# First eight units: v and q scaled three units ahead, one load queue, scores from scaled q with a mask

## The chip, the cores and the metric

One NeuronCore of a Trainium2 chip runs the whole program. The metric is the device time of one execution in microseconds, the median of the runs. The engines are TensorE (PE, with its weight loads as PEld), VectorE (DVE), ScalarE (ACT), GpSimd (POOL), and SP, which here only issues DMAs; each has its own queue of instructions and they meet through semaphores.

## The reference

Three parts, one after the other. A linear attention with decay on q, k, v of 4 batches, 8 heads, 768 positions, 64 dimensions:

```python
state = gamma * state + k[t] (outer) v[t]      # gamma = 1 - 2**(-5 - head)
y[t]  = q[t] @ state / sqrt(64)
```

Its output, 3072 tokens of 512, goes through `h = x @ w_in; g = h - tanh(h); y = g @ w_out` with 2048 inner columns, and that through a second such block with 1024 inner columns: `h = x @ w_in2`, softmax of h times h, a layer norm with the gain g_ln, and `@ w_out2`. All weights and the output are float32 on the outside; the weights of the first and second block come as float64 words, which the kernel turns into float32.

## The kernel before, in words

The attention is worked in chunks of 128 positions. Chunk c and batch b are one unit, k = 4c + b, so there are 24 units in six chunks, and a unit holds all 8 heads. Inside a unit the chunk is split in two halves of 64 positions. For each unit two tiles `z` of 512 KB come from memory: one with q and k, dimensions on the partitions, one with k and v, positions on the partitions. Decay is taken out of the recurrence by scaling: v is multiplied by gamma to the power of minus its position (`vs`, constants in `con`), q by gamma to the power of its position over 8 (`qs`, constants in a table `tab` of 256 KB per chunk). `prepare` makes both. `unit(ko, ks)` does the outputs of unit ko (`out`: scaled q against the states, L240 to L244, and the kept scores against v, L245 to L251) and the scores and state products of unit ks (`sc`: k against q, and k against v, L278 to L286). Scores go through VectorE into `pr`, where they are multiplied by a second table, which holds the decay and the causal mask at once (L290). States are `sa` and `sb`. The outputs are summed into `xf` (ScalarE copies L262 to L266, VectorE adds L268) and split into a high part rounded to the matmul format (`xh`, L306) and the low rest (`xl`, L307), in the tile `xt` of the chunk.

A matmul of float32 shows in the trace as two instructions; a score or output product is 64 x 64 by 64 columns, a product of the dense blocks 128 x 128 by 512 columns.

The first dense block works on one chunk of four units (512 tokens) at a time. `step_h(n, b)` takes column block n of 16 for chunk b: twelve matmuls `ph` (L319), tanh on ScalarE (L325), the difference on VectorE (L326). The weights of each block n are decoded from their words in four stages by the class Decoder: load (`raw`, SP's queue), absolute value on ScalarE (L121), four VectorE operations (L128 to L135), and the split into high and low (L144, L145). `dec1.to(stage, upto)` runs one stage up to a number of blocks.

The program for the first two chunks is at L382 to L412: units 0 to 7, with the scores two units ahead of the outputs, `prepare` two ahead, and one `step_h` at k = 4. Then the loop from L414 runs the h steps of chunks 0 and 1 with units 8 to 11 among them, then the y products (`py`, L343) of both chunks, then from L489 chunks 2 to 5, with the units 12 to 23 as visits between the steps (L494 to L500), and at last the second dense block.

Program order sets priorities; a list scheduler with its own model of times then orders each engine's queue, and moves loads forward where a buffer is free. Tiles come from two pools of equal buffers: `t4` (44 of 4 KB a partition: z, raw, w, xt, g) and `t2` (17 of 2 KB: vs, qs, tab, pr, xf, wf and others). `products` keeps the order of the small matmuls among themselves. In the kernel before, z, w_in and con are issued from SP's queue and the tables from ScalarE's.

Of the kernel before, what the change touches and what calls it, by code (L numbers as in the profile page):

```python
# [57 lines left out]

C_VS = 0
C_HALF = C_VS + NC * H  # L60
C_IDENT = C_HALF + 1
C_END = C_IDENT + P


# [5 lines left out]
def constants():  # L70
    gamma = 1.0 - 2.0 ** (-5.0 - np.arange(H, dtype=np.float64))
    i = np.arange(P, dtype=np.float64)
    out = np.zeros((P, C_END), np.float64)
    out[:, C_IDENT : C_IDENT + P] = np.eye(P)
    for c in range(NC):
        out[:, C_VS + c * H : C_VS + (c + 1) * H] = gamma[None, :] ** -(c * P + i[:, None] + 1)
    out[:, C_HALF] = -0.5

    tab = np.zeros((NC, 2, P, 4 * P), np.float64)
    of_score = tab[:, 0].reshape(NC, 2, D, 2, NP, D)  # L80
    of_q = tab[:, 1].reshape(NC, 2, D, NP, P)
    for p in range(NP):
        for h in range(2):
            for c in range(NC):
                t = gamma[2 * p + h] ** (c * P + i + 1) / np.sqrt(D)
                of_q[c, h, :, p, :] = t
                of_score[c, :, :, h, p, :] = t.reshape(2, 1, D) * (i[:D, None] <= i[None, :D])
    return out.astype(np.float32), tab.astype(np.float32)


# [1 line left out]
def body(ctx: ExitStack, tc, z, w_in, w_out, w_in2, w_out2, g_ln, cst, tab, out):  # L92
# [8 lines left out]
    def t4(shape, dtype, name):  # L101
        return big.tile(shape, dtype, tag="t4", name=name)

    def t2(shape, dtype, name):
        return mid.tile(shape, dtype, tag="t2", name=name)

    con = cpool.tile([P, C_IDENT], F32, name="con")
    gl = cpool.tile([P, NF2], F32, name="gl")
    mhalf = con[:, C_HALF : C_HALF + 1]
    y1d = [yd.tile([P, B, NK, P], F32, name=f"y1d{s}") for s in range(NSB)]  # L110


# [67 lines left out]
    xc = {}  # L180
    loaded = [0]

    def load_units(upto):
        while loaded[0] < min(upto, NU):
            k = loaded[0]
            if k % B == 0:
                tb[k // B] = [t2([P, NP * P], F32, "tab") for _ in range(2)]
                for n, t in enumerate(tb[k // B]):
                    nc.scalar.dma_start(out=t, in_=tab[k // B, n])
            for half, to in ((0, zq), (1, zv)):  # L190
                t = t4([P, 2, NP, P], F32, "z")
                nc.sync.dma_start(out=t.rearrange("p a b c -> p (a b c)"), in_=z[2 * k + half])
                to[k] = t
            loaded[0] += 1

    def rows(h):
        return slice(h * D, (h + 1) * D)
# [4 lines left out]
                nc.tensor.matmul(o, a, b, start=True, stop=True, skip_group_check=True)  # L202
            )

    def prepare(k, own):

        c = k // B
        v = t2([P, H, D], F32, "vs")
        src = zv[k][:, 1, :, :].rearrange("q p (h d) -> q (p h) d", h=2)
        c0 = C_VS + c * H  # L210
        for h in range(own):
            nc.scalar.activation(
                v[:, h, :], src[:, h, :], AF.Copy, scale=con[:, c0 + h : c0 + h + 1]
            )
        if own < H:
            nc.gpsimd.tensor_tensor(  # L216
                v[:, own:, :], src[:, own:, :],
                con[:, c0 + own : c0 + H].unsqueeze(2).to_broadcast([P, H - own, D]), ALU.mult,
            )
        vs[k] = v  # L220
        qs[k] = t2([P, NP, P], F32, "qs")
        nc.gpsimd.tensor_tensor(
            qs[k].rearrange("q p t -> q (p t)"),
            zq[k][:, 0, :, :].rearrange("q p t -> q (p t)"), tb[c][1], ALU.mult,
        )

    def unit(ko, ks, hold=False, pool=ps_r, tag="r", engs=None):


        if ko is not None:  # L230
            c, b = divmod(ko, B)
            q, v, po, st = qs.pop(ko), vs.pop(ko), pt.pop(ko), (sa.pop(ko, None), sb.pop(ko))
            w = [ps_r.tile([P, 2, 4 * D], F32, tag="r", name="out") for _ in range(2)]
            fr = [t[:, 0, :].rearrange("q (i t) -> q i t", i=2) for t in w]
            y = [t[:, 1, :].rearrange("q (h i t) -> q h i t", h=2, i=2) for t in w]

            steps = range(2) if c else (1,)
            products([
                (
                    fr[h][rows(col(2 * i + odd, h)), i, rows(ab)],  # L240
                    st[ab][rows(h), 2 * i + odd, :], q[rows(h), 2 * i + odd, rows(ab)],
                )
                for i in range(2) for ab in steps for odd in range(2) for h in range(2)
            ])  # L244
            products([  # L245
                (
                    y[ab][rows(col(p, h)), h, p // 2, :], v[rows(ab), 2 * p + h, :],
                    po[rows(ab), h, p, :],
                )
                for p in range(NP) for ab in range(2) for h in range(2)  # L250
            ])  # L251
            if hold:
                if b % 2 == 0:
                    xc[b // 2] = t4([P, 2, 2, 2, P], F32, "xc")
                xf = xc[b // 2][:, b % 2, :, :, :]
            else:
                xf = t2([P, 2, 2, P], F32, "xf")
            xa = xf.rearrange("q h i t -> q (h i) t")
            ya = [t.rearrange("q h i t -> q (h i) t") for t in y]
            if c:  # L260
                for h in range(2):
                    nc.scalar.copy(xf[:, h, :, :], fr[h])  # L262
            else:
                for h in range(2):
                    nc.scalar.copy(xf[:, h, :, rows(1)], fr[h][:, :, rows(1)])
                nc.scalar.copy(xa[:, :, rows(0)], ya[0])  # L266
            for ab in steps:
                nc.vector.tensor_tensor(  # L268
                    xa[:, :, rows(ab)], xa[:, :, rows(ab)], ya[ab], ALU.add
                )  # L270
            if not hold:
                split_x(c, b, xf, engs or (nc.gpsimd, nc.gpsimd))
        if ks is not None:
            c = ks // B
            kq, kv, v = zq[ks], zv.pop(ks), vs[ks]
            w = [pool.tile([P, 2, 4 * D], F32, tag=tag, name="sc") for _ in range(2)]
            sc, gn = ([t[:, n, :].rearrange("q (p t) -> q p t", p=NP) for t in w] for n in range(2))
            products([  # L278
                (sc[h][rows(ab), p, :], kq[rows(h), 1, p, rows(ab)], kq[rows(h), 0, p, rows(ab)])
                for p in range(NP) for h in range(2) for ab in range(2)  # L280
            ])
            zq.pop(ks)
            products([
                (gn[ab][rows(h), p, :], kv[rows(ab), 0, p, rows(h)], v[rows(ab), 2 * p + h, :])
                for p in range(NP) for ab in range(2) for h in range(2)
            ])  # L286
            pr = t2([P, 2, NP, D], F32, "pr")
            for h in range(2):
                f = tb[c][0].rearrange("q (h p t) -> q h p t", h=2, p=NP)[:, h, :, :]
                nc.vector.tensor_tensor(pr[:, h, :, :], sc[h], f, ALU.mult)  # L290
            pt[ks] = pr
            sb[ks] = stp.tile([P, NP, D], F32, tag="sb", name="sb", bufs=3)
            if c == 0:
                nc.scalar.copy(sb[ks], gn[0])
            else:
                nc.vector.tensor_tensor(sb[ks], sa[ks], gn[0], ALU.add)
            if c < NC - 1:
                sa[ks + B] = stp.tile([P, NP, D], F32, tag="sa", name="sa")
                nc.vector.tensor_tensor(sa[ks + B], sb[ks], gn[1], ALU.add)
# [80 lines left out]


    spare = dict(pool=ps_y, tag="y")  # L382
    both = dict(engs=(nc.vector, nc.gpsimd))
    dec1.n = NF1
    load_units(1)
    nc.sync.dma_start(out=con, in_=cst[:, :C_IDENT])
    load_units(2)
    dec1.to(0, 1)
    load_units(5)
    prepare(0, H // 2)  # L390
    unit(None, 0, **spare)
    prepare(1, H // 2)
    for st in range(1, 4):
        dec1.to(st, 1)
    unit(None, 1, **spare)
    g2 = {}

    def step_h(n, b):
        if b == 0:
            g2[n] = t4([P, 2, SB], F32, "g")  # L400
        less_tanh(products_h(b, n, ps_y, "y"), g2[n][:, b, :])

    for k in range(2 * B):
        load_units(min(k + 6, 2 * B))
        if k + 2 < 2 * B:
            prepare(k + 2, H // 2)
        if k == B:
            step_h(0, 0)
        unit(k, k + 2 if k + 2 < 2 * B else None, **both, **(spare if k < B else {}))
        if k >= B:  # L410
            dec1.to(0, k - B + 2)
    dec1.step()  # L412
    nc.sync.dma_start(out=gl, in_=g_ln)
    for n in range(NF1):  # L414
        while dec1.at[3] < n + 1:
            dec1.step()
        for b in range(2):
            if n or b:
                step_h(n, b)

        if LATER <= n <= LATER + B:
# [234 lines left out]
```

## Time and profile before

| | us |
|---|---|
| median of 3 runs | 909.95 (909.57 to 910.24) |
| the profiled execution's own time | 910.57 |
| its span (first to last instruction) | 908.8 |
| TensorE busy | 876.0 |

The span is 1.8 us less than the profiled execution's time; that execution was 0.62 us above the median. The rows further down are from this one execution; their times count from the start of the span. "Idle before, with a releaser" names what ended the wait of an engine; "issue" stands for time in which the engine waited for nothing that the profile shows.

### The profile page before, as it was taken

The page shows a single profiled execution, that of the slowest core. Times are in us where ns is not written, and L with a number is a line of the kernel's source. Part 1 is how long each engine was busy: PE and PEld are TensorE (multiplying, and loading weights), DVE is VectorE, ACT ScalarE, POOL GpSimd, SP SyncE. Part 2 cuts the span into 40 slices and gives each one's busy share as a digit, 9 for nine tenths or more (in the row PEclk, how much of TensorE's full clock was granted, in tenths as well). Part 3 has the DMA queues.
Part 4 walks back from the last instruction along what each step waited for, and adds up shares of the span by engine and source line. Part 5 has one row for each costly group of instructions (what it writes and reads, how often), then busy time and mean ns, then how long its engine had stood idle before and what let it go on. Part 6 is the DMA issues. An engine that isn't in the chain of part 4 may idle for free.

```text
span 908.8 us, 15882 instructions
## 1 busy us (share of the span) xinstructions
PE 876.0 (96%) x6656; PEld 724.9 (80%) x6656; DVE 429.9 (47%) x872; ACT 300.7 (33%) x605; POOL 195.9 (22%) x200
## 2 busy tenths in 40 slices
PE   5669999999999999999999999999999999999998
PEld 4558887888888888888888888888888888888886
DVE  3466876994223233222322259964544444444442
ACT  4435544652111112111211134522433333333332
POOL 3422000000044333333333310010322112222210
PEclk9779999999999999999999999999999999999999
DMA  9913203422411313110311046114111111000000
GB/s 357 408 77 116 72 25 118 138 72 90 116 47 57 107 48 94 48 60 11 100 41 47 25 128 196 48 38 136 31 40 46 47 47 46 24 24 24 24 25 35
DMA packets 35640, 73.47 MB, mean 81 GB/s; under 512 B 3184, under 2 KB 15600, under 8 KB 35568
## 3 DMA queue, kind: packets, MB, share of 16 engines
q1 hardware_dynamic: 17712, 56.73, 18.5%
q10 hardware_dynamic: 17856, 15.73, 5.5%
q8 instruction: 52, 0.85, 0.4%
q14 instruction: 20, 0.16, 0.1%
HBM read 59.86 MB, written 12.58 MB: 80 GB/s over the span
## 4 chain that ended last, share of the span: by engine, by line
PE 90%; issue 3%; DVE 2%; POOL 2%; ACT 2%; DMA 1%; POOLq 0%; DVEq 0%; ACTq 0%
PE ph L319 29%; PE py L343 26%; PE po L580 14%; PE ph L532 14%; PE ptr L567 2%; PE sc L202 2%; PE out L202 2%; POOL vs L216 1%; DVE g L326 1%; ACT th L325 1%; DMA z<-z 1%; POOL xl L307 1%; DMA tab<-tab 1%; DVE gh L333 0%; DVE xf L268 0%
## 5 line engine op out<-in xcount | busy, mean ns | idle before, releaser
L319 PE MATMUL ph<-xh,w 128*128 128x512 f32 x768 | 248.1, 392 | 5.3 <-ACT xh L306 4.9
L343 PE MATMUL py<-gh,w 128*128 128x512 f32 x768 | 248.2, 391 | 1.2 <-ACT gh L331 1.2
L319 PEld LDWEIGHTS ph<-xh,w 128*128 128x128 f32 x768 | 144.7, 188 | 36.5 <-ACT xh L306 5.3
L343 PEld LDWEIGHTS py<-gh,w 128*128 128x128 f32 x768 | 144.1, 188 | 32.1 <-ACT gh L331 1.6
L326 DVE TENSOR_TENSOR g<-ph,th 128x512 f32<-128x512 f32 x96 | 66.2, 690 | 196.4 <-ACT th L325 196.4
L319 PE MATMUL ph<-xl,w 128*128 128x512 f32 x384 | 150.3, 391 | 0.1
L343 PE MATMUL py<-gl,w 128*128 128x512 f32 x384 | 149.8, 390 | 0.0
L325 ACT ACTIVATE th<-ph 128x512 f32<-128x512 f32 x96 | 57.3, 599 | 257.4 <-PE ph L319 244.5
L532 PE MATMUL ph<-w,y 128*128 128x512 f32 x576 | 134.8, 389 | 0.0
L334 POOL TENSOR_TENSOR gl<-g,gh 128x512 fp32r<-128x512 f32 x48 | 61.8, 1287 | 329.3 <-DVE gh L333 305.3
L532 PEld LDWEIGHTS ph<-w,y 128*128 128x128 f32 x576 | 108.0, 188 | 22.4
L580 PE MATMUL po<-w,uh 128*128 128x512 f32 x384 | 120.4, 395 | 0.0
L378 POOL TENSOR_TENSOR y<-yl,y 128x512 fp32r<-128x512 f32 x24 | 42.2, 1759 | 260.9 <-ACT y L377 260.9
L538 DVE TENSOR_REDUCE nmx<-ph 128x1 f32<-128x1024 f32 x24 | 29.4, 1225 | 117.7 <-PE ph L532 117.7
L319 PEld LDWEIGHTS ph<-xl,w 128*128 128x128 f32 x384 | 72.5, 189 | 15.7 <-POOL xl L307 0.5
L343 PEld LDWEIGHTS py<-gl,w 128*128 128x128 f32 x384 | 72.1, 188 | 14.8
L580 PEld LDWEIGHTS po<-w,uh 128*128 128x128 f32 x384 | 70.5, 188 | 13.6
L580 PE MATMUL po<-w,ul 128*128 128x512 f32 x192 | 75.3, 392 | 0.0
L541 ACT ACTIVATE ex<-ph,nmx 128x1024 f32<-128x1024 f32 x24 | 26.8, 1117 | 132.5 <-DVE nmx L538 132.5
L543 DVE SCALAR_TENSOR_TENSOR ex<-ph,ex 128x1024 f32<-128x1024 f32 x24 | 29.4, 1225 | 29.8 <-ACT ex L541 29.8
L580 PEld LDWEIGHTS po<-w,ul 128*128 128x128 f32 x192 | 36.0, 188 | 7.6
L334 DVE TENSOR_TENSOR gl<-g,gh 128x512 fp32r<-128x512 f32 x48 | 33.7, 708 | 8.8 <-PE py L343 5.5
(63 smaller groups left out, 848.8 us busy)
## 6 DMA issues: line engine op xcount, KB each, us to landing
z<-z SPq DMA_DIRECT2D x48, 512.0 KB, 5.8
raw<-w_in SPq DMA_DIRECT2D x24, 512.0 KB, 5.0
raw<-w_out SPq DMA_DIRECT2D x24, 512.0 KB, 3.7
y1d<-ysb ACTq DMA_DIRECT2D x24, 256.0 KB, 3.6
yl<-y1d SPq DMA_DIRECT2D x24, 256.0 KB, 3.2
out<-ob ACTq DMA_DIRECT2D x24, 256.0 KB, 2.3
tab<-tab ACTq DMA_DIRECT2D x12, 256.0 KB, 4.6
ident<-cst SPq DMA_DIRECT2D x1, 64.0 KB, 9.2
```

Of the source, the lines that this page charges most:

```text
L202: nc.tensor.matmul(o, a, b, start=True, stop=True, skip_group_check=True)
L319: nc.tensor.matmul(ph, a[:, k, :], x, start=n == 0, stop=n == 3 * NK - 1)
L325: nc.scalar.activation(th, ph, AF.Tanh)
L326: nc.vector.tensor_tensor(g, ph, th, ALU.subtract)
L334: eng_l.tensor_tensor(gl_, g, gh.bitcast(F32), ALU.subtract)
L343: nc.tensor.matmul(py[e], a[:, cols], x, start=f == 0 and n == 0, stop=f == NF1 - 1 and n == 2)
L378: nc.gpsimd.tensor_tensor(yo, t, yh.bitcast(F32), ALU.subtract)
L532: nc.tensor.matmul(ph[:, half, :], a[:, k, :], b, start=n == 0, stop=n == 3 * NK - 1)
L538: nc.vector.tensor_reduce(nmx, phf, AX.X, ALU.max, negate=True)
L541: nc.scalar.activation(ex, phf, AF.Exp, bias=nmx, scale=1.0, accum_out=ssum)
L543: nc.vector.scalar_tensor_tensor(ex, phf, 1.0, ex, ALU.mult, ALU.mult, accum_out=us)
L580: nc.tensor.matmul(po, a[:, f, :], b, start=n == 0, stop=n == 3 * NF2 - 1)
```

## The change

Tables: the two tables per chunk become one, for q alone. The scores are now taken from the scaled q, so that what is left of the second table is the causal mask, 64 columns in `con`, read with a broadcast over the four head pairs. Loads: the tables are issued from SP's queue instead of ScalarE's, and the first loads are written in one order: the q and k tile of unit 0, table 0, con, the k and v tile of unit 0, units 1 and 2, the first w_in, units 3 to 5, the second w_in, table 1, units 6 and 7. `prepare` does q first and then v, and for the first eight units puts both in one 4 KB buffer of `t4`; it runs three units ahead instead of two. A tanh on one column at the very start brings ScalarE's table load there. Among the visits, the decode stages of w_in blocks 0 and 1 are written out at k = 1, 2 and 4, 5, and two h steps stand there: (0, 0) at k = 4 and (1, 0) at k = 6. The subtraction L307 of unit 7 is done by VectorE for both halves (units 0 to 6: one half each on VectorE and POOL). All small products of the score part now take their accumulators from the pool of the y products.

```diff
--- before.py
+++ after.py
@@ -58,7 +58,8 @@
 
 C_VS = 0
 C_HALF = C_VS + NC * H
-C_IDENT = C_HALF + 1
+C_MASK = C_HALF + 1
+C_IDENT = C_MASK + D
 C_END = C_IDENT + P
 
 
@@ -75,16 +76,14 @@
     for c in range(NC):
         out[:, C_VS + c * H : C_VS + (c + 1) * H] = gamma[None, :] ** -(c * P + i[:, None] + 1)
     out[:, C_HALF] = -0.5
-
-    tab = np.zeros((NC, 2, P, 4 * P), np.float64)
-    of_score = tab[:, 0].reshape(NC, 2, D, 2, NP, D)
-    of_q = tab[:, 1].reshape(NC, 2, D, NP, P)
+    out[:, C_MASK : C_MASK + D] = np.tile(i[:D, None] <= i[None, :D], (2, 1))
+
+    tab = np.zeros((NC, P, NP * P), np.float64)
+    of_q = tab.reshape(NC, 2, D, NP, P)
     for p in range(NP):
         for h in range(2):
             for c in range(NC):
-                t = gamma[2 * p + h] ** (c * P + i + 1) / np.sqrt(D)
-                of_q[c, h, :, p, :] = t
-                of_score[c, :, :, h, p, :] = t.reshape(2, 1, D) * (i[:D, None] <= i[None, :D])
+                of_q[c, h, :, p, :] = gamma[2 * p + h] ** (c * P + i + 1) / np.sqrt(D)
     return out.astype(np.float32), tab.astype(np.float32)
 
 
@@ -107,6 +106,7 @@
     con = cpool.tile([P, C_IDENT], F32, name="con")
     gl = cpool.tile([P, NF2], F32, name="gl")
     mhalf = con[:, C_HALF : C_HALF + 1]
+    mask = con[:, C_MASK : C_MASK + D]
     y1d = [yd.tile([P, B, NK, P], F32, name=f"y1d{s}") for s in range(NSB)]
 
 
@@ -180,17 +180,22 @@
     xc = {}
     loaded = [0]
 
+    def load_tab(c):
+        tb[c] = t2([P, NP * P], F32, "tab")
+        nc.sync.dma_start(out=tb[c], in_=tab[c])
+
+    def load_half(k, half):
+        t = t4([P, 2, NP, P], F32, "z")
+        nc.sync.dma_start(out=t.rearrange("p a b c -> p (a b c)"), in_=z[2 * k + half])
+        (zv if half else zq)[k] = t
+
     def load_units(upto):
         while loaded[0] < min(upto, NU):
             k = loaded[0]
-            if k % B == 0:
-                tb[k // B] = [t2([P, NP * P], F32, "tab") for _ in range(2)]
-                for n, t in enumerate(tb[k // B]):
-                    nc.scalar.dma_start(out=t, in_=tab[k // B, n])
-            for half, to in ((0, zq), (1, zv)):
-                t = t4([P, 2, NP, P], F32, "z")
-                nc.sync.dma_start(out=t.rearrange("p a b c -> p (a b c)"), in_=z[2 * k + half])
-                to[k] = t
+            if k // B not in tb:
+                load_tab(k // B)
+            for half in range(2):
+                load_half(k, half)
             loaded[0] += 1
 
     def rows(h):
@@ -202,10 +207,20 @@
                 nc.tensor.matmul(o, a, b, start=True, stop=True, skip_group_check=True)
             )
 
-    def prepare(k, own):
+    def prepare(k, own, wide=False):
 
         c = k // B
-        v = t2([P, H, D], F32, "vs")
+        if wide:
+            t = t4([P, 2, H * D], F32, "vq")
+            v = t[:, 0, :].rearrange("q (h d) -> q h d", h=H)
+            qs[k] = t[:, 1, :].rearrange("q (p t) -> q p t", p=NP)
+        else:
+            v = t2([P, H, D], F32, "vs")
+            qs[k] = t2([P, NP, P], F32, "qs")
+        nc.gpsimd.tensor_tensor(
+            qs[k].rearrange("q p t -> q (p t)"),
+            zq[k][:, 0, :, :].rearrange("q p t -> q (p t)"), tb[c], ALU.mult,
+        )
         src = zv[k][:, 1, :, :].rearrange("q p (h d) -> q (p h) d", h=2)
         c0 = C_VS + c * H
         for h in range(own):
@@ -218,11 +233,6 @@
                 con[:, c0 + own : c0 + H].unsqueeze(2).to_broadcast([P, H - own, D]), ALU.mult,
             )
         vs[k] = v
-        qs[k] = t2([P, NP, P], F32, "qs")
-        nc.gpsimd.tensor_tensor(
-            qs[k].rearrange("q p t -> q (p t)"),
-            zq[k][:, 0, :, :].rearrange("q p t -> q (p t)"), tb[c][1], ALU.mult,
-        )
 
     def unit(ko, ks, hold=False, pool=ps_r, tag="r", engs=None):
 
@@ -272,22 +282,22 @@
                 split_x(c, b, xf, engs or (nc.gpsimd, nc.gpsimd))
         if ks is not None:
             c = ks // B
-            kq, kv, v = zq[ks], zv.pop(ks), vs[ks]
+            kt, kv, v, q = zq.pop(ks)[:, 1, :, :], zv.pop(ks), vs[ks], qs[ks]
             w = [pool.tile([P, 2, 4 * D], F32, tag=tag, name="sc") for _ in range(2)]
             sc, gn = ([t[:, n, :].rearrange("q (p t) -> q p t", p=NP) for t in w] for n in range(2))
             products([
-                (sc[h][rows(ab), p, :], kq[rows(h), 1, p, rows(ab)], kq[rows(h), 0, p, rows(ab)])
+                (sc[h][rows(ab), p, :], kt[rows(h), p, rows(ab)], q[rows(h), p, rows(ab)])
                 for p in range(NP) for h in range(2) for ab in range(2)
             ])
-            zq.pop(ks)
             products([
                 (gn[ab][rows(h), p, :], kv[rows(ab), 0, p, rows(h)], v[rows(ab), 2 * p + h, :])
                 for p in range(NP) for ab in range(2) for h in range(2)
             ])
             pr = t2([P, 2, NP, D], F32, "pr")
             for h in range(2):
-                f = tb[c][0].rearrange("q (h p t) -> q h p t", h=2, p=NP)[:, h, :, :]
-                nc.vector.tensor_tensor(pr[:, h, :, :], sc[h], f, ALU.mult)
+                nc.vector.tensor_tensor(
+                    pr[:, h, :, :], sc[h], mask.unsqueeze(1).to_broadcast([P, NP, D]), ALU.mult
+                )
             pt[ks] = pr
             sb[ks] = stp.tile([P, NP, D], F32, tag="sb", name="sb", bufs=3)
             if c == 0:
@@ -380,19 +390,11 @@
 
 
     spare = dict(pool=ps_y, tag="y")
-    both = dict(engs=(nc.vector, nc.gpsimd))
     dec1.n = NF1
-    load_units(1)
-    nc.sync.dma_start(out=con, in_=cst[:, :C_IDENT])
-    load_units(2)
-    dec1.to(0, 1)
-    load_units(5)
-    prepare(0, H // 2)
-    unit(None, 0, **spare)
-    prepare(1, H // 2)
-    for st in range(1, 4):
-        dec1.to(st, 1)
-    unit(None, 1, **spare)
+
+    warm = cpool.tile([P, 1], F32, name="warm")
+    nc.gpsimd.memset(warm, 0.0)
+    nc.scalar.activation(warm, warm, AF.Tanh)
     g2 = {}
 
     def step_h(n, b):
@@ -400,22 +402,41 @@
             g2[n] = t4([P, 2, SB], F32, "g")
         less_tanh(products_h(b, n, ps_y, "y"), g2[n][:, b, :])
 
+    load_half(0, 0)
+    load_tab(0)
+    nc.sync.dma_start(out=con, in_=cst[:, :C_IDENT])
+    load_half(0, 1)
+    loaded[0] = 1
+    load_units(3)
+    dec1.to(0, 1)
+    load_units(6)
+    dec1.to(0, 2)
+    load_units(2 * B)
+    prepare(0, H // 2, True)
+    prepare(1, H // 2, True)
+    unit(None, 0, **spare)
+    prepare(2, H // 2, True)
+    unit(None, 1, **spare)
     for k in range(2 * B):
-        load_units(min(k + 6, 2 * B))
-        if k + 2 < 2 * B:
-            prepare(k + 2, H // 2)
-        if k == B:
-            step_h(0, 0)
-        unit(k, k + 2 if k + 2 < 2 * B else None, **both, **(spare if k < B else {}))
-        if k >= B:
-            dec1.to(0, k - B + 2)
-    dec1.step()
+        if k + 3 < 2 * B:
+            prepare(k + 3, H // 2, True)
+        both = (nc.vector, nc.gpsimd) if k < 2 * B - 1 else (nc.vector, nc.vector)
+        unit(k, k + 2 if k + 2 < 2 * B else None, engs=both, **spare)
+
+        if k in (1, 4):
+            for st in (1, 2):
+                dec1.to(st, 1 + (k > 1))
+        elif k in (2, 5):
+            dec1.to(3, 1 + (k > 2))
+        if k in (4, 6):
+            step_h((k - 4) // 2, 0)
+    dec1.to(0, 4)
     nc.sync.dma_start(out=gl, in_=g_ln)
     for n in range(NF1):
         while dec1.at[3] < n + 1:
             dec1.step()
         for b in range(2):
-            if n or b:
+            if n > 1 or b:
                 step_h(n, b)
 
         if LATER <= n <= LATER + B:
```

## Rows read from the trace of the kernel before

**Rows 1.** Page, part 1: busy time (share of the span) and instructions, by engine.
```profile
PE 876.0 (96%) x6656; PEld 724.9 (80%) x6656; DVE 429.9 (47%) x872; ACT 300.7 (33%) x605; POOL 195.9 (22%) x200
```

**Rows 2.** Windows: stretch, length, busy us per engine, PE clock, DMA share, GB/s.
```profile
2.00:12.00 10.00, 3.32 (x96) 3.14 (x96) 0.54 (x2) 2.43 (x6) 2.32 (x3) 1.00 0.99 372
49.00:61.40 12.40, 6.99 (x130) 5.30 (x129) 9.13 (x20) 5.53 (x13) 5.06 (x2) 0.59 0.07 26
61.40:905.00 843.60, 841.24 (x5674) 695.18 (x5674) 401.75 (x805) 274.21 (x523) 171.31 (x172) 1.00 0.20 64
```

**Rows 3.** Waits of PE, whole span: waiter, releaser, us in total, times, longest.
```profile
PE out L202 <- issue: 8.5, 3, 3.2
```

**Rows 4.** The chain of waits, 20 to 84 us: start, length, what.
```profile
21.34 2.66 issue
...
27.69 2.58 issue
...
33.30 3.29 PE ph L319 x12
36.60 1.11 PE out L202 x64
...
39.66 3.16 issue
...
46.35 2.73 issue
...
57.02 4.35 POOL xl L307
...
61.41 22.10 PE ph L319 x96
```

**Rows 5.** Windows of the first 43 us, columns as in group 2.
```profile
5.00:17.50 12.50, 8.26 (x221) 7.50 (x221) 4.44 (x10) 5.91 (x17) 5.82 (x6) 1.00 1.03 407
17.50:23.90 6.40, 3.28 (x127) 2.70 (x127) 3.39 (x8) 4.98 (x20) 3.93 (x7) 0.91 1.03 399
30.20:42.70 12.50, 8.96 (x252) 7.40 (x253) 5.36 (x14) 5.31 (x18) 5.17 (x7) 0.89 1.03 407
```

**Rows 6.** Page, part 3, whole span: queue, packets, MB, share of 16 engines.
```profile
q8 instruction: 52, 0.85, 0.4%
```

**Rows 7.** DMA queues and issues of 0 to 50 us (issues: count, size, landing).
```profile
q1 hardware_dynamic: 5295, 17.81, 90.8%
...
q8 instruction: 6, 0.10, 0.8%
...
z<-z SPq DMA_DIRECT2D x24, 512.0 KB, 8.0
raw<-w_in SPq DMA_DIRECT2D x10, 512.0 KB, 9.8
```

**Rows 8.** Timeline, ACT and POOL, 8 to 10 us.
```profile
8.11 1.28 ACT L212 ACT_TABLE_LOAD   x1 [8.11 <-DMA con<-cst]
...
8.75 1.26 POOL L222 TENSOR_TENSOR qs<-z,tab 128x512 f32<-128x512 f32 x1
```

**Rows 9.** Timeline, PE and DVE, 56 to 58 us.
```profile
56.69 0.79 PE L319 MATMUL ph<-xh,w 128*128 128x512 f32 x1 [4.92 <-ACT xh L306]
...
57.94 0.42 DVE L307 TENSOR_TENSOR xl<-xf,xh 128x256 fp32r<-128x256 f32 x1
```

**Rows 10.** Timeline, ACT, 39 us (unit 4).
```profile
39.26 0.71 ACT L306 CAST xh<-xf 128x256 fp32r<-128x256 f32 x2 [0.87 <-DVE xf L268]
```

**Rows 11.** Timeline, a visit of the fourth chunk or later, 401 to 403 us.
```profile
401.69 1.04 POOL L216 TENSOR_TENSOR vs<-z,con 128x512 f32<-128x512 f32 x1
...
401.98 0.65 PE L202 MATMUL sc<-z 64*64 64x64 f32 x32
...
402.69 1.28 POOL L222 TENSOR_TENSOR qs<-z,tab 128x512 f32<-128x512 f32 x1
...
402.78 0.40 PE L202 MATMUL sc<-vs,z 64*64 64x64 f32 x12 [0.16 <-POOL vs L216]
```

## The prediction

> **What bounds the kernel now.** I read the page first, then the windows, the waits, the chain, and last the DMA queues. The page [rows 1] has TensorE busy 876.0 us, 96% of the span. The windows [rows 2] show where the difference lies: from 61.40 us to 905 us TensorE is busy 841.24 of 843.60 us at full clock, so 2.4 us can be had there; from 49.00 to 61.40 us it is busy 6.99 us of 12.40 at a granted clock of 0.59. Nearly everything this change can give is in the first 61 us, and anything it loses after that is paid in full.
>
> In those 61 us the eight units of the first two chunks run. TensorE's own wait list [rows 3] has 8.5 us in three waits on "issue" at the products of the outputs, with nothing in the profile that it waited for. The chain [rows 4] has these, and one more ahead of them, in order: 2.66 us from 21.34, then 2.58, 3.16 and 2.73 us, the last from 46.35; they end at 24.00, 30.27, 42.82 and 49.08 us, which is 6.27, 2 x 6.27 and 6.26 us apart. The windows count the instructions [rows 5]: 127 matmuls with 127 weight loads in the 6.4 us before 23.90, and 252 with 253 in the two blocks from 30.20 to 42.70. The page's instruction queue carried 52 packets and 0.85 MB [rows 6] for 6656 matmuls and 6656 weight loads [rows 1]: 13312 / 52 = 256 instructions a packet. So each stall comes after one packet's worth of TensorE's own program, and ends when the next packet is there. In the first 50 us that queue moved 6 packets while the load queue took 90.8% of the DMA engines' time [rows 7]. My reading: **in this stretch TensorE is bound by its instruction supply, one block of some 127 matmuls per 6.27 us, while loads fill the DMA engines.** A unit of the second chunk is 64 output and 64 score and state instructions, 128, so a unit costs 6.27 us whatever its data does. The one block without a stall (ending near 36.5 us) holds twelve long matmuls of an h step, 3.29 us [rows 4], which hid the rest of the fetch.
>
> The loads that keep the engines full are not those of the eight units: 24 z tiles and 10 of w_in are issued in 50 us [rows 7], of which the units need 16 and one. At about 405 GB/s (399 to 407 in [rows 5]), the first 16 tiles, one w_in and the tables (10 MB) are in by some 27 us: 3.7 MB by 12 us at the 372 GB/s of [rows 2], the rest in 15.5 us.
>
> The Trainium skill ("Runtime: NRT & Kernel Launch", Instruction fetch mechanics) says that the program is streamed in 16 KiB blocks of 256 instructions, and that crossing a block is mostly hidden. The block size agrees with the 256 above; that it is hidden does not hold here before 50 us [rows 4]. By that rule the units would be free to run at the pace of their data, which is rival C below.
>
> **The change part by part.**
>
> *Loads in one queue.* The tables drop from four to two of 256 KB before unit 7, and come in SP's queue between z tiles. That is 0.52 MB less ahead of the last unit: 1.3 us at 405 GB/s, of no use while instructions are late. con grows by 64 columns (some 32 KB, 0.1 us). Nothing in the edit stops SP from going on to the w_in and z tiles of later stages after unit 7. What it might meet is a buffer: the wide tiles (v and q together) now take eight buffers of the 44-buffer pool, so some loads behind unit 7 will wait for a release. I take the engines as full until about 45 us, as now; ends: 34 us (SP stops after seven w_in, 12.5 MB) and 55 us (it goes on).
>
> *Start.* Before, the table load of ScalarE, 1.28 us, starts at 8.11 us when con has landed [rows 8], POOL's first qs starts at 8.75 us. After, the warm-up takes the table load to the front, con comes after 0.8 MB, and v of unit 0 after 1.4 MB, near 6 us; scores now wait for q scaled on POOL (1.26 us), so they start near 6.4 us where before they started as the first tile landed. Unit 1's scores want its q: 1.9 MB, near 7.3 us by the same rate, plus POOL, near 9 us. The first block boundary (some 93 matmuls in: 221 by 17.50 us in [rows 5], less 128) is then reached about 2.1 us sooner; bounds 0 and 4. Each later block is asked for when its predecessor starts, so the whole ladder 24.0 ... 49.1 moves by this: last block near 46.9 us.
>
> *Scores from scaled q, mask instead of a table.* The DVE product has the same size, PSUM by SBUF: 0; bounds plus or minus 0.1 us a unit, hidden under 6.27.
>
> *h steps among the visits.* Step (0,0) was there already; (1,0) is new there. Twelve matmuls at 22.10/96 = 0.23 us [rows 4] are 2.76 us taken out of the later, saturated stretch. But it stands ahead of the last unit's outputs in TensorE's order, in the last block: 49 short matmuls, the step, then 64. A short one is 17 ns at full clock (1.11 us for 64, [rows 4]), so 113 of them and the step are 1.9 + 2.8 us, or twice that at half clock: the outputs of unit 7 end at 51.6 to 56.3 us. I take 53.3, since the step before, at 33.30, took 3.29 us rather than 5.5 [rows 4]. Before: 56.69 - 4.92 = 51.8 [rows 9].
>
> *End of the stretch.* Before, the first h product starts at 56.69 us, 4.92 us after the outputs [rows 9], because ScalarE had w_in stages in between and VectorE too; then POOL's subtraction of the low half takes 4.35 us from 57.02 [rows 4] beside VectorE. Now both halves are VectorE's, 0.42 us each [rows 9]. The clean chain, from unit 4: outputs from 36.60 for 1.11 us [rows 4], cast at 39.26 us, 0.71 us for two halves [rows 10]: about 2.1 us from the outputs to the first half, and so to the first product. If the decode steps still stand between, 4.9. I take 2.1.
>
> *Sum.* Before: ten h products were done by 61.41, so full rate is worth 61.4 - 2.3 = 59.1. After: 53.3 + 2.1 + 0.7 (clock not yet full; 0 to 1.4) - 2.76 = 53.3. **Gain 5.8 us**; with the outputs of unit 7, the chain and the clock at their ends, 0 to 8.2, and with the start's bounds up to 10.
>
> *Later visits, 12 of them from 250 to 500 us.* At one of them POOL does vs at 401.69 (1.04 us), then qs (1.28 us); the scores start at 401.98, before vs is ready, and the state products wait 0.16 us [rows 11]. Now qs comes first and the scores need it: at 402.97 rather than 401.98, and the state products at 404.0 rather than 402.78. Cover: the twelve y products behind them, 2.7 us, which may be put in front. With cover a tenth or less per visit, without it 1.3 us x 12 = 15. I take 0.5 in all, nearer the covered end, since TensorE's idle time from 61.40 to 905 us is 2.4 us in all [rows 2] with the same kind of wait in it; bounds -1.9 (12 x 0.16 gone) and +15.
>
> 909.95 - 5.8 + 0.5 = **904.6** for the median; the profiled execution's 910.57 stands 0.6 above it.
>
> **Rivals.**
>
> A. As above, instructions bind until the end of the stretch: 904.6, own range 901 to 907.5. Chance 0.50.
>
> B. SP meets a buffer wait and the engines empty at 34 to 40 us. The last one or two blocks then come in some 3 us: 4 to 8 us more: 896 to 901. For it: eight more buffers taken. Against: the early z buffers are free by then. 0.16.
>
> C. The instruction supply is no limit, or goes with the new queue order. Then data and engines set the pace: 0.52 x 2 MB / 405 GB/s = 2.6 us a unit, unit 7 landed at 27, plus q, scores, mask, outputs and cast, some 8 us, plus an h step: full rate worth 38 - 2.8 = 35 at best, 24 us gained; with half of the slack lost, 17. About 889. Against it: the equal spacing of the stalls, which no data shows. 0.10. By the skill's rule above it would be this one.
>
> D. Nothing to speak of: the start's 2.1 us are lost on the scores' new wait for POOL, and the step that moved only delays the last outputs by its own 2.8. 908.2 to 911. 0.12.
>
> E. Slower: the later visits' scores wait on qs uncovered, 1.28 us at each of 12. 15.4 - 5.8: 919.5. It decides from 0.5 us a visit on. For it: order qs before vs, products kept in order; against: y products at hand. 0.12.
>
> **Numbers.** I forecast A. What a measurement here can tell from no change is 0.2%, 1.8 us. Faster: A, B, C and a little: 0.77; same 0.11; slower 0.12. The range 893 to 909.5 holds A, B and most of D; C and E are left out.
>
> **What would show it.** Stalls on "issue" still about 6.3 us apart, 127 matmuls between, starting some 2 us earlier; h products going by 55 to 56 us; no 4 us subtraction on POOL at the end; waits on POOL qs at the scores of later visits below 0.2 us. I am wrong if the stalls vanish (C), if loads stop before 40 us (B), or if TensorE waits on qs after 250 us (E).

## The result and the profile after

The changed kernel takes 920.26 us (918.71 to 920.85), the kernel before 909.83 beside it: ratio 1.0112, 95% interval 1.0094 to 1.0129, so about 10 us slower. The profiled execution has a span of 918.1 us, against 908.8.

The list of TensorE's waits of the changed kernel answers to [rows 3]; columns: waiter, releaser, us in total, times, longest.

```profile
PE sc L207 <- POOL vq L220: 7.0, 2, 6.5
PE out L207 <- ACT sb L304: 5.7, 1, 5.7
PE ph L329 <- ACT w L144: 5.5, 1, 5.5
PE out L207 <- issue: 3.9, 2, 2.9
...
PE sc L207 <- POOL qs L220: 1.1, 2, 0.7
```

Windows of the changed kernel, columns as in [rows 2]:

```profile
30.00:43.00 13.00, 8.11 (x233) 7.04 (x233) 8.31 (x20) 7.08 (x24) 4.24 (x5) 0.63 0.75 296
49.00:61.40 12.40, 9.82 (x100) 7.25 (x98) 6.16 (x15) 4.61 (x13) 3.98 (x4) 1.00 0.83 319
61.40:905.00 843.60, 832.00 (x5607) 686.05 (x5608) 403.86 (x811) 272.31 (x521) 168.23 (x170) 0.99 0.20 62
...
61.40:66.74 5.34, 0.00 (x0) 0.00 (x0) 5.26 (x13) 2.15 (x5) 0.00 (x0) 0.78 0.25 98
66.74:72.00 5.26, 5.26 (x14) 4.16 (x15) 5.16 (x8) 1.14 (x2) 1.34 (x1) 0.57 0.34 100
```

From 49.00 to 61.40 us TensorE does more than before (9.82 us busy against 6.99, at full clock instead of 0.59). After that it is idle 11.6 us, where before it was 2.4 [rows 2]. So the change did bring its gain, and it was lost behind it. The h products count it. Windows limited to the tile `ph` (the first count in each line is TensorE's matmuls), first of the changed kernel, then of the kernel before:

```profile
0.00:61.30 61.30, 13.07 (x48) 9.47 (x48) 1.92 (x3) 1.78 (x3) 0.89 0.80 308
0.00:76.00 76.00, 22.33 (x79) 16.91 (x80) 3.45 (x5) 3.38 (x6) 0.87 0.71 269
0.00:120.00 120.00, 53.95 (x205) 41.32 (x206) 10.98 (x16) 9.29 (x16) 0.90 0.51 189
```

```profile
0.00:61.30 61.30, 7.59 (x22) 4.97 (x22) 0.69 (x1) 0.60 (x1) 0.81 0.81 312
0.00:76.00 76.00, 22.18 (x86) 17.04 (x87) 4.14 (x6) 3.75 (x7) 0.84 0.65 252
0.00:120.00 120.00, 57.94 (x235) 44.39 (x236) 12.80 (x19) 11.25 (x19) 0.90 0.52 195
```

By 61.3 us it is 48 products against 22: 26 at 0.23 us are **6.0 us ahead**. By 76 us it is 79 against 86, and by 120 us, when both kernels have the third chunk's units behind them, 205 against 235.

The timeline of the changed kernel shows where that goes (start, length, instruction; in brackets the idle time before it and what ended it):

```profile
18.55 0.71 PE L207 MATMUL out<-vq,sb 64*64 64x64 f32 x16 [5.71 <-ACT sb L304]
...
26.32 0.28 PE L207 MATMUL sc<-vq,z 64*64 64x64 f32 x3 [2.09 <-issue]
32.49 0.28 PE L207 MATMUL out<-vq,sb 64*64 64x64 f32 x3 [2.90 <-issue]
38.77 0.38 PE L207 MATMUL out<-vq,sb 64*64 64x64 f32 x4 [0.99 <-issue]
...
54.89 1.29 DVE L317 TENSOR_TENSOR xl<-xf,xh 128x256 fp32r<-128x256 f32 x2 [0.53 <-ACT xh L316]
54.91 0.73 PE L329 MATMUL ph<-xh,w 128*128 128x512 f32 x2 [2.15 <-ACT xh L316]
...
60.13 0.60 ACT L335 ACTIVATE th<-ph 128x512 f32<-128x512 f32 x1 [4.96 <-PE ph L329]
60.63 1.77 ACT L121 ACTIVATE wf<-raw 128x512 f32<-128x512 f32 x3
...
66.74 0.79 PE L329 MATMUL ph<-xh,w 128*128 128x512 f32 x1 [5.52 <-ACT w L144]
...
90.84 0.69 PE L207 MATMUL sc<-qs,z 64*64 64x64 f32 x32
...
91.82 0.30 PE L207 MATMUL out<-qs,sa 64*64 64x64 f32 x8
92.87 0.34 PE L207 MATMUL out<-qs,sb 64*64 64x64 f32 x8 [0.75 <-DVE sb L306]
...
97.65 0.76 PE L207 MATMUL out<-qs,sa 64*64 64x64 f32 x8 [2.55 <-DVE xc L278]
...
161.98 2.11 PE L353 MATMUL py<-gh,w 128*128 128x512 f32 x8 [1.19 <-ACT gh L341]
```

And of the kernel before, rows not shown so far:

```profile
83.44 0.69 PE L202 MATMUL sc<-z 64*64 64x64 f32 x32
...
90.65 0.34 PE L202 MATMUL out<-qs,sa 64*64 64x64 f32 x8
...
155.30 2.12 PE L343 MATMUL py<-gh,w 128*128 128x512 f32 x8 [1.19 <-ACT gh L331]
```

The first y product follows all 384 h products of chunks 0 and 1, so its start is a mark that every version shares: 155.30 before, 161.98 after. Of the 9.3 us between the spans 6.7 are lost by then, and 2.6 behind it. With the 6.0 us gained, 12.7 us go between 61 and 162 us, in two places. **First**, at 61.22 TensorE has nothing to do for 5.52 us, until ScalarE has cast the weights of the third block of w_in; then the granted clock is low (0.57 from 66.74 to 72.00, so mostly at the lower of its two levels, 1.2 and 2.4 GHz). From 61.3 to 76 us 33 products are lost, 7.6 us. ScalarE's absolute values for that block (L121, at 60.63) stand right behind the tanh of h step (0, 1), at 60.13. In the kernel before, `dec1.step()` took that block on before the loop; the change has `dec1.to(0, 4)` there, which only loads. **Second**, in the third chunk the scores of unit 8 (90.84) stand right in front of its outputs (91.82), where before 7.2 us and 26 h products lay between. TensorE waits 0.75 us for the state and 2.55 us for sums, and the clock falls once more (0.74 from 97.65 to 104.25 us). From 76 to 120 us 23 products are lost, 5.3 us.

### The profile page after: what moved, and what is told of

It is laid out like the page before. It is cut to its first block, busy times and chain, and to the rows that moved or that the text cites. A ratio compares the mean times of both kernels' runs of the same rounds, so it can differ in the third digit from the quotient of the medians.

```text
span 918.1 us, 15885 instructions
## 1 busy us (share of the span) xinstructions
PE 878.7 (96%) x6656; PEld 725.5 (79%) x6656; DVE 432.4 (47%) x873; ACT 300.5 (33%) x606; POOL 192.3 (21%) x200
## 4 chain that ended last, share of the span: by engine, by line
PE 92%; DMA 3%; ACT 1%; DVE 1%; issue 1%; SPq 1%; POOL 1%; ACTq 0%; POOLq 0%; DVEq 0%
PE py L353 28%; PE ph L329 28%; PE po L601 14%; PE ph L553 14%; PE out L207 3%; PE sc L207 2%; PE ptr L588 2%; DMA z<-z 1%; DMA raw<-w_in 1%; DMA y1d<-ysb 1%; SPq L189 0%; ACT vq L227 0%; POOL qs L220 0%; DVE wf L135 0%; ACT th L335 0%
## 5 line engine op out<-in xcount | busy, mean ns | idle before, releaser
L298 DVE TENSOR_TENSOR pr<-sc,con 128x256 f32<-128x256 f32 x48 | 19.8, 419 | 44.4 <-PE sc L207 44.4
```

## The experiments

My theory: the dropped `dec1.step()` and the scores from scaled q in the third chunk make the loss, and the visits a little. Rivals: loads that come late; SP's queue, which the table of the third chunk holds from some 32.5 to 50.07 us until a t2 buffer is free; the visits alone, as in rival E; the wide tiles. Line numbers differ a little from kernel to kernel.

| kernel | median, us | before beside it | ratio, 95% interval | span | first y product |
|---|---|---|---|---|---|
| the change | 920.26 | 909.83 | 1.0112 (1.0094 to 1.0129) | 918.1 | 161.98 |
| e1 decode step back | 915.08 | 910.75 | 1.0048 (1.0033 to 1.0063) | 912.4 | 156.32 |
| e4 tables on ScalarE's queue | 922.65 | 910.75 | 1.0133 (1.0118 to 1.0148) | 920.2 | 164.19 |
| e6 old scores, q still first | 927.31 | 910.75 | 1.0185 (1.017 to 1.02) | 926.9 | 164.16 |
| e7 before, with scaled scores | 918.27 | 910.75 | 1.0086 (1.0069 to 1.0104) | 916.9 | 162.69 |
| e8 old scores, v first | 912.48 | 910.99 | 1.0017 (1.0006 to 1.0029) | 909.8 | 156.12 |
| e9 e1, scaled scores for 8 units | 905.66 | 910.99 | 0.9942 (0.9927 to 0.9957) | 903.3 | 148.69 |
| e10 e9, later loads held | 908.31 | 910.99 | 0.9968 (0.9955 to 0.9981) | 906.3 | 152.80 |
| e11 e9, two ahead, small tiles | 900.97 | 910.99 | 0.9896 (0.9879 to 0.9912) | 898.7 | 145.21 |
| two ahead, wide tiles | 902.65 | 910.46 | 0.9907 (0.989 to 0.9923) | 901.7 | 147.76 |
| e12 scaled scores for 12 units | 913.2 | 910.46 | 1.0025 (1.0015 to 1.0034) | 911.1 | 156.51 |

**The decode step put back (e1).**

```diff
-    dec1.to(0, 4)
+    dec1.step()
     nc.sync.dma_start(out=gl, in_=g_ln)
```

> The changed kernel, in which one call is put back behind the loop of the eight units: a whole decode step, which takes the third block of w_in through all four stages there, instead of its load alone. Theory 'three places' (the changed kernel loses 8.6 us where TensorE waits at 61 to 67 us for the third block, 5.2 us in the third chunk at 80 to 116 us, 2.4 us in the later visits): 911.5 to 914, no wait of h products on the weights at 61 us. Rival 'loads' (the table of the third chunk stops SP's queue from 32.5 to 50 us, and the weights come late for that): 918 to 921, the wait stays.

ScalarE's timeline in e1:

```profile
53.42 0.68 ACT L121 ACTIVATE wf<-raw 128x512 f32<-128x512 f32 x1
...
58.53 0.62 ACT L144 CAST w<-wf 128x512 fp32r<-128x512 f32 x1 [2.21 <-DVE wf L135]
```

The block is taken up at 53.42 instead of 60.63, its cast comes at 58.53, and the wait is gone from the list. The mark moves by 5.66 us, and by the ratios the time falls by 5.8; the median lies 1.1 us above the range expected. In its first 61.3 us e1 is behind the changed kernel (40 h products against 48; its stalls on "issue" sum to 8.1 us against 6.0, which no run explains). By 76 us it has 105 against 79, so between the two 34 products come back, 7.8 us: the wait and the low clock behind it. e1 is still slower than the kernel before by 0.5%: the edit is one cause, not the whole.

**Tables back on ScalarE's queue (e4).** With SP free, the loads behind the table are issued early.

```diff
-        nc.sync.dma_start(out=tb[c], in_=tab[c])
+        nc.scalar.dma_start(out=tb[c], in_=tab[c])
```

> The changed kernel with the tables issued from ScalarE's queue as in the kernel before, all else as changed. 'Three places': 918.5 to 921.5, the wait on the third block at 61 us as it was. 'Loads': 910 to 913, since SP's queue is no longer stopped at 32.5 us; the wait goes.

922.65 is 1.2 us above the first range and far from the second. The timeline of e4, SP's queue, TensorE and ScalarE:

```profile
42.65 0.33 SPq L115 DMA_DIRECT2D raw<-w_in  x1
...
50.69 0.28 PE L207 MATMUL out<-vq,sb 64*64 64x64 f32 x3 [2.95 <-issue]
...
62.56 0.60 ACT L335 ACTIVATE th<-ph 128x512 f32<-128x512 f32 x1 [4.39 <-PE ph L329]
63.05 1.77 ACT L121 ACTIVATE wf<-raw 128x512 f32<-128x512 f32 x3
```

SP's last w_in before 70 us is issued at 42.65 now, not behind 50.07, and still ScalarE takes the block up behind the tanh; the wait of 5.5 us stands in the list as before. So ScalarE's order makes it, not the load. The rival of the loads falls. In the changed kernel's own chain a load of w_in (54.05 to 63.20) stands on the path, but in e4's chain that place is taken by the tanh at 62.56 and the absolute values at 63.05, with no load. e4 shows one thing more: with SP free the DMA engines stay busy (share 0.84 from 38.0 to 50.7 us, 0.13 in the changed kernel), and a fourth stall on "issue" is there, 2.95 us long, where the changed kernel has none.

**Unscaled scores throughout (e6, e8).** The score part of the kernel before, with its two tables. In e6 `prepare` still does q ahead of v; e8 puts v first again.

```diff
-            kt, kv, v, q = zq.pop(ks)[:, 1, :, :], zv.pop(ks), vs[ks], qs[ks]
+            zz, kv, v = zq.pop(ks), zv.pop(ks), vs[ks]
+            kt, q = zz[:, 1, :, :], zz[:, 0, :, :]
...
+                f = tb[c][0].rearrange("q (h p t) -> q h p t", h=2, p=NP)[:, h, :, :]
+                nc.vector.tensor_tensor(pr[:, h, :, :], sc[h], f, ALU.mult)
```

> The changed kernel with the scores taken again from the unscaled q and multiplied by the second table (so two tables a chunk, in SP's queue). 'Three places': the third chunk and the later visits give back 5.2 and 2.4 us, 912 to 914; the wait at 61 us stays. 'Loads': twice the table bytes in the queue that stalls, 920 to 923.

This missed by 13 us: 927.31. TensorE's waits and its timeline in e6 name it:

```profile
PE sc L211 <- POOL vs L235: 7.8, 11, 0.8
```

```profile
86.97 0.69 PE L211 MATMUL sc<-z 64*64 64x64 f32 x32
...
93.03 0.69 PE L211 MATMUL sc<-vs,z 64*64 64x64 f32 x32
93.55 0.30 PE L211 MATMUL out<-qs,sa 64*64 64x64 f32 x8
...
99.91 0.67 PE L211 MATMUL out<-qs,sa 64*64 64x64 f32 x8 [3.07 <-DVE xc L282]
```

In the visits only v is needed by the state products now, and it stands behind q on POOL: eleven waits, 7.8 us. That is one half: from the mark to the end e6 takes 762.7 us, e8 below 753.7. The other 8.0 us lie in front of the mark, and the third chunk has its share of them although the scores take the raw q: the state products of unit 8 (93.03) stand right in front of its outputs (93.55), 6.1 us behind its scores, and the wait for sums is there (3.07 us). By 76 us e6 has 73 h products and e8 84, by 120 us 196 and 231: 24 of them, 5.5 us, are lost in the third chunk. So q ahead of v in `prepare` brings the third chunk's loss without scaled scores. The order inside `prepare` and the scores' operand belong together. With v first:

> The changed kernel with the whole score part as before: scores from the unscaled q, two tables, and in prepare v ahead of q. Theory 'scores need q': it is the wait for the scaled q, and q ahead of v on POOL, that moves the scores in the third chunk right in front of their outputs (5.2 us) and costs 2.4 us in the later visits: 912 to 914, the lag behind the kernel before no longer growing from 80 to 116 us. Rival 'load order': the third chunk's loss comes from the loads and the late weights: 918 to 921.

912.48, as expected; the same list for e8 has 0.6 us in four such waits, while the 5.5 us for the weights are still there.

```profile
PE ph L333 <- ACT w L147: 5.5, 1, 5.5
```

**The scaled scores alone, in the kernel before (e7).** One table, on ScalarE's queue as there; all the rest as before, v ahead of q too.

```diff
-  (sc[h][rows(ab), p, :], kq[rows(h), 1, p, rows(ab)], kq[rows(h), 0, p, rows(ab)])
+  (sc[h][rows(ab), p, :], kt[rows(h), p, rows(ab)], q[rows(h), p, rows(ab)])
```

> The kernel before with one part of the change alone: scores from the scaled q with the mask (one table a chunk, from ScalarE's queue), all else as before. 'Three places': 5.2 and 2.4 us lost, 915.5 to 918. 'Loads': 909 to 911, nothing in the loads has changed but 1 MB less of tables.

918.27: 7.5 us slower by this edit alone, 0.3 above the range expected. Its timeline has the third chunk of the changed kernel again:

```profile
90.26 0.69 PE L201 MATMUL sc<-qs,z 64*64 64x64 f32 x32
...
91.24 0.30 PE L201 MATMUL out<-qs,sa 64*64 64x64 f32 x8
...
97.50 0.91 PE L201 MATMUL out<-qs,sa 64*64 64x64 f32 x8 [2.98 <-DVE xc L267]
```

The mark is 7.4 us late, and from it to the end of the span there are 754.2 us against 753.5 before: the loss lies in front of the visits. By 76 us e7 is 4 h products behind the kernel before (82 against 86), by 120 us 33 (202 against 235): some 6.7 us are lost in the third chunk. So either part is enough to bring that loss, scaled scores (e7) or q ahead of v (e6).

**Scaled scores for the first eight units only, decode step back (e9).** From unit 8 on v is ahead of q again.

```diff
+        if c < 2:
+            scale_q()
...
+                if c < 2:
+                    f = mask.unsqueeze(1).to_broadcast([P, NP, D])
+                else:
+                    f = tb[c][0].rearrange("q (h p t) -> q h p t", h=2, p=NP)[:, h, :, :]
```

> The changed kernel with the decode step put back, and scores from scaled q with the mask for the first eight units alone; from unit 8 on scores from the unscaled q with the second table, v ahead of q. 'Three places': nothing of the three losses is left, and the lead of 4.2 us that the first of these runs had at 75 us is kept to the end: 904.5 to 908. Rival 'lead given back': the decode work or the units of the third chunk take it back on VectorE: 909 to 912.

905.66. The timeline of e9 has the old order of the third chunk, with 6.0 us from the start of one unit's scores to its outputs, and no wait at either:

```profile
85.13 0.66 PE L212 MATMUL sc<-z 64*64 64x64 f32 x32
...
91.17 0.35 PE L212 MATMUL out<-qs,sa 64*64 64x64 f32 x8
```

**The same for the first twelve units (e12).** The limit of chunks moves by one (`c < 2` becomes `c < 3`): the third chunk scaled, the visits not. With it q comes ahead of v there, and the chunk's second table is not loaded.

> Scores of the first twelve units from scaled q with the mask; from unit 12 on as in the kernel before; the rest as in the split kernel with eight such units, which took 905.66 us. My theory (in the third chunk, with the scaled scores, unit 8's scores stand directly in front of its outputs and TensorE waits, some 5 us; the visits 12 to 23 cost 2 to 3 us by waits on POOL): about 910.5 (909 to 912), with the waits on VectorE's sb and xc in the third chunk back, and no wait of scores on POOL after 250 us. Rival (the visits carry most of the loss of the scaled scores, or the tables' loads do): 905 to 908.

913.2, 7.5 us above e9 and 1.2 above the range expected. The timeline of e12:

```profile
85.39 0.69 PE L212 MATMUL sc<-qs,z 64*64 64x64 f32 x32
...
86.37 0.30 PE L212 MATMUL out<-qs,sa 64*64 64x64 f32 x8
...
92.21 0.76 PE L212 MATMUL out<-qs,sa 64*64 64x64 f32 x8 [2.55 <-DVE xc L290]
```

The order of the changed kernel and its two waits (0.75 us for the state, 2.55 for sums) are back, the mark moves by 7.82 us, and from the mark to the end there are 754.6 us, as in e9. Not all of the 7.82 us belong to the third chunk: by 61.3 us e12 has 39 h products and e9 50, by 76 us 103 and 115, by 120 us 229 and 264. So 12 products, 2.8 us, are lost before the third chunk's units, which no run explains, and 23, 5.3 us, in it, as many as in the changed kernel. In the changed kernel the visits add some 1.5 us more (756.1 from the mark to the end, 754.6 here).

**Loads behind unit 7 held (e10).** e9, with a tiny write into five raw tiles that waits for unit 7's result.

```diff
+        if held[0] and 1 in xt:
+            nc.gpsimd.tensor_copy(raw[:1, 0, 0:1].bitcast(F32), xt[1][0][0][:1, 0, 0:1].bitcast(F32))
+            held[0] -= 1
```

> As the run beside it with the split scores, and the loads behind unit 7 (w_in from the third block on, and with them the z tiles of the third chunk, which stand behind in SP's queue) held until the second chunk's first unit is cast: one element of each of five w_in tiles is written by POOL from that unit's result ahead of its load. Theory 'instructions behind loads': once the first eight units' data are in, at some 27 us, the DMA engines are idle and TensorE's waits on issue end with them; unit 7's outputs end at 45 to 48 us instead of 52.5; 900 to 904 unless the held weights come late. Rival 'stalls of their own': the stalls of 2 to 3 us every 127 matmuls go on without loads: 905 to 908.

Half right. A window and the timeline of e10:

```profile
27.50:50.00 22.50, 16.50 (x515) 14.22 (x505) 17.80 (x40) 10.10 (x32) 7.77 (x8) 0.85 0.04 11
```

```profile
30.11 0.28 PE L218 MATMUL out<-vq,sb 64*64 64x64 f32 x3 [1.60 <-issue]
34.90 0.33 PE L218 MATMUL out<-vq,sa 64*64 64x64 f32 x2 [3.03 <-ACT xf L294]
...
56.64 1.22 PE L350 MATMUL ph<-xh,w 128*128 128x512 f32 x2 [5.23 <-ACT xh L337]
```

From 27.5 us the DMA engines are nearly idle (share 0.04), and after 30.11 no stall on "issue" is left in some 450 matmuls. But the units do not end at 45 to 48 us: TensorE now waits for ScalarE's and VectorE's work on the outputs, which end at 51.4 us (53.1 in e9). Then it waits 5.23 us for the cast, which stands on ScalarE behind the absolute values of a held block (at 55.63, when its load has landed): the held weights come late. With the low clock behind it (0.50 from 56.64 to 62.00 us) that costs more than was won.

**Two units ahead, with small tiles (e11) and with the wide ones.** e9 with the distance of the kernel before; the wide version keeps `True` as the last argument.

```diff
-        if k + 3 < 2 * B:
-            prepare(k + 3, H // 2, True)
+        if k + 2 < 2 * B:
+            prepare(k + 2, H // 2)
```

> As the run with the split scores, and v and q of the first eight units in separate small tiles and two units ahead, as in the kernel before; ScalarE's queue then has the first state copy ahead of the fourth unit's v. TensorE's wait of 6 us at 12 to 19 us goes. Theory 'instructions behind loads': the blocks of instructions arrive every 6.3 us from the first boundary on, and starting sooner is worth 0 to 3 us: 903 to 907. Rival 'order': the whole wait is gained, 899 to 902.

> The split kernel (905.66 us) with prepare two units ahead instead of three, but v and q still together in one 4 KB buffer. The kernel with both (two ahead, separate small tiles) took 900.97. If the distance is the cause (at three ahead ScalarE has sixteen copies of v of four units in front of the first state copy, and TensorE's first outputs wait for it): 900 to 902.5, and no wait of 5 us on ScalarE's sb. If the wide buffers are (they take eight of the pool of 44 and hold back or reorder loads): 904.5 to 906.

900.97 and 902.65. The first falls into the rival's range, not into my theory's: the whole wait is gained. The second is 0.15 us above the range for the distance. TensorE's waits in the wide version, and in e11:

```profile
PE out L212 <- ACT sb L319: 1.9, 1, 1.9
```

```profile
PE sc L212 <- issue: 5.4, 2, 2.8
PE out L212 <- issue: 4.3, 3, 2.4
```

At three ahead the first outputs wait 5.7 us (6.9 in e9) for the copy of the first state, because the scaling of v of four units, the last of them landed at 17.15 us, is in front of it on ScalarE. Two ahead takes that to 1.9 us, small tiles to nothing. The stalls move with the start: the first one ends at 23.24 us in the wide version, at 26.82 in e9. By the ratios some 3 of the 4.2 us come from the distance; the rest, 1.0 us between the two versions, is not clear of the noise. e11 is the fastest version of all, 1.0% below the kernel before, with 9.7 us of stalls on "issue" still in it.

## Why the prediction was wrong

It forecast 904.6 us. Its terms for the end of the stretch held, and two things that it left out cost more than all of them gave.

- *End of the stretch*: the first h product comes 2.15 us behind the outputs (2.1 forecast), both low halves on VectorE by 56.2 us, nothing on POOL.
- *h step (1, 0)*: twelve products from 48.73 in 2.94 us (2.76), the last unit's outputs from 51.60 to 52.85 (53.3). The gain at 61 us was 6.0 us where the sum has 5.8.
- *Start*: wrong in sign. The first stall ends at 26.32 us, 2.3 later than before, not 2.1 earlier, because of ScalarE's order in front of the first outputs. It was made good by what rival B said: SP met a buffer (one of t2, for the table of the third chunk, not one of the 44 that rival B had in mind), the DMA engines went empty near 40 us (share 0.75 from 30 to 43), and the ladder ends: 26.32, 32.49, 38.77, the familiar 6.2 and 6.3 us apart, then no stall. So it is luck that the outputs of unit 7 ended so near to the 53.3 us of the sum: two misses made up for each other.
- *The step that failed first* is the costing of the edits itself: the replacement of `dec1.step()` by `dec1.to(0, 4)` stands in the diff and has neither a word in the text on the change nor a term in the sum. It was taken for loads alone. "Full rate" from 53.3 us on needs weights of a third block, and nothing in the sum made them. It cost 7.6 us between 61.3 and 76 us, and e1, which puts the call back, gains 5.7 us at the mark.
- *The step that failed second*: the scores from scaled q were costed for the eight units (0) and for twelve visits (0.5). The four units of the third chunk, 8 to 11, were in neither. They lost 5.3 us there in the changed kernel, and as much from e9 to e12; in the kernel before scaled scores alone cost some 6.7 (e7). The price is not the scaled scores' alone: q ahead of v, the other half of the same edit, brings the loss too (e6), and was priced for the visits only. The step "cover: y products, which may be put in front" was right for the visits in its mechanism, as at the visit of 409 us eight y products now stand between the outputs and the scores; but some 1.5 to 2.6 us went there, above the 0.5. In the third chunk the order went the other way: products that had stood behind the scores were moved in front of them, and the chain from the scores to the outputs lay open. No run shows why the scheduler's model did so. In the trace neither operand was late: POOL had scaled the q of units 8 and 9 by 55.6 us and ScalarE their v by 85.0, and the scores start at 90.84.

Rival E had the sign and, by luck, nearly the size (919.5), for another cause: the waits of the visits' scores on POOL's q are 1.1 us in all, not 15. With both failed steps undone, e9 takes 905.66, within 1.1 us of the forecast; that is in part luck too, since its start is as late as the changed kernel's and its visits are the old ones.

Rival C falls. The Trainium skill ("Runtime: NRT & Kernel Launch", Instruction fetch mechanics) has block crossings mostly hidden: here stalls are there while loads fill the engines in every version, each with its own order of the work, up to 4.07 us long (e1), and they end with the loads in e10. It holds, then, near enough for idle DMA engines only: with share 0.00 the longest stall is 0.75 us (two ahead, wide tiles, from 44.60), and e10's last one, 1.60 us, falls into the end of the loads (share 0.06). That the late thing is the instruction packet itself is inferred from this and from the count of 256; no row shows TensorE's sequencer waiting for one.

## What to carry to other kernels

Walk through the diff line by line and give each line a term, also the one that looks like bookkeeping: a removed call that seemed to be about loads was the one that started the next block's work. When an operand of an operation changes, list every place that runs it, by stage, and look in each for the distance between producer and consumer; a scheduler may close it without any wait showing in the rows at first. And where the gain is real but given back, put a mark that all versions share, such as the first y product, and read each version against it.

## What the runs showed of the hardware

With the DMA engines nearly idle (share 0.01 from 30.2 to 50.0 us in e10), some 450 matmuls passed without a stall on "issue". With full engines, the kernel before stalls 2.58 to 3.16 us after four of the five packets' worth of instructions that end from 24 to 49 us; in the fifth a step of twelve long matmuls stands. And a pause of TensorE costs more than its own length: after the 5.52 us of idle time in the changed kernel the granted clock was 0.57 for 5.26 us, in which 14 matmuls of the dense block took what some 23 take at 0.23 us.
